# Two attention layers between two long convolutions: a written instruction order per step, one exp over four PSUM banks, turns by DMA and GpSimd, first blocks by predicated copies

## The chip, the cores and the metric

The kernel runs on one core of a Trainium2 chip. The metric is the time of one launch in device microseconds (us), the median over a kernel's runs. Every ratio below is the mean time of one kernel's fast runs over the mean of the other's fast runs of the same rounds, with a 95% interval; it is therefore not quite the ratio of the medians that stand beside it. Shares and durations come from one profiled run of each kernel. The engines are PE (matmul; PEld is its weight load), DVE (vector), ACT (scalar), POOL (GpSimd) and SP (the queue that issues most DMAs).

## The reference, cut to what matters

```python
x = A_u                                             # 1 x 2048 x 512, bf16
x = x + _A_ref(_layernorm(x), A_..., )              # long convolution over 2048 positions
x = x + _B_ref(_layernorm(x), B_wqkv, B_wo)         # attention 1
x = x + _A_ref(_layernorm(x), A_..., )              # the same convolution again
x = x + _B_ref(_layernorm(x), B_wqkv, B_wo)         # attention 2, the same weights

def _B_ref(x, wqkv, wo):
    H = 32; Dh = 16; W, dil = 8, 2                  # each query sees 8 keys, two apart
    q, k, v = split(x @ wqkv)
    logits = q . k[pos - 2*(0..7)] * Dh**-0.5       # masked before position 0
    o = softmax(logits) @ v
    return o @ wo
```

Keys are two positions apart, so even and odd positions never meet. The kernel treats them as two parities. It cuts each parity into blocks of 114 queries against 128 keys, with a mask added in the matmul. One step handles 16 (head, block) pairs, and there are 36 steps in each attention layer.

## The kernel before

One attention layer normalises X, turns it (channels to partitions), projects to K and Q, and then runs 36 steps. A step makes logits on PE, takes exp on ACT, multiplies by V on PE and divides on DVE. Projections for later steps are pulled from a queue during the steps.

```python
def start(g):                       # four row tiles: norm, turn on PE, copy out of PSUM
    for i in range(4):
        ln_b.norm(xn[i][:], X[:, slot(g * 4 + i), :], g * 4 + i)                # DVE, L212
    for ch in range(2):
        pt = gps([128, 4, 2, 128], BF)
        # ... eight nc.tensor.transpose, then copies on ACT and DVE into xnT
def proj(n, k):                     # 512 positions of 128 features of K or Q
    # ... four matmuls of 512 columns (L941), copy to st[n] (L943)
    if h:                           # a DMA spreads st over the two halves of K or Q
        for e in range(2):
            nc.sync.dma_start(T[e::2, e, f2, UF:UF + 1024], st[n][e::2, :])
def logits(t):
    for ih in range(2):
        S4 = psS.tile([128, 2, 512], F32, name="S4", tag="S4")       # two banks, two buffers
        # ... eight matmuls (L968)
        nc.scalar.activation(pt[:, ih*8*NQ:(ih+1)*8*NQ]..., S4[:, :, 0:4*NQ], ACT.Exp, scale=DH**-0.5)   # L971
def values(t):                      # 16 matmuls with V (L985), reciprocal, multiply to on (DVE)
    ...
def turn_o(t):                      # two PE transposes a step, one DVE copy every third step
    ...
for g in range(2): start(g)
for k in range(4): proj(0, k)       # whole first K/Q before the first step
for g in range(2, 4): start(g)
queue = [ ... proj, vproj, out ... ]
for t in range(N + LT):
    logits(t)
    # ... as many jobs of the queue as pace(t) allows
    values(t - 2); turn_o(t - 4)
for m in range(8, 16): out(m)       # output projection; statistics for the next layer per 4 rows
```

The order of instructions on the engines was left to the scheduler here. Convolution 2 began by normalising X into U by groups of four rows, and turned its first blocks (`zt<-Z`) by a DMA transpose.

Of the kernel before, what the change touches and what calls it, by code (L numbers as in the profile page):

```python
# [18 lines left out]
S = 2048  # L19
# [23 lines left out]
HALO = 7  # L43
MASK = 2048.0
# [116 lines left out]
def load_b_weights(nc, const, wq_in, C, wqkv, wo):  # L161
    wqk = const.tile([128, 4, 1024], BF, name="wqk")
    wv = const.tile([128, 4, 512], BF, name="wv")
    wo_t = const.tile([128, 4, 512], BF, name="wo_t")
    wsrc = wqkv.rearrange("(t p) f -> p t f", p=128)
    eng = nc.gpsimd
    mask = nc.inline_tensor(_bf(_mask_rows()), name="c_mask").ap()
    sets = []
    for u in range(2):
        sets.append([const.tile([128, 2, 2, UW], BF, name=f"{nm}{u}") for nm in ("KS", "QS")])  # L170
        for w, T in enumerate(sets[u]):
            nc.gpsimd.memset(T[:, :, :, 0:UF], 0.0)
            nc.gpsimd.memset(T[:, :, :, UF + 1024:UW], 0.0)
            for e in range(2):
                eng.dma_start(T[1 - e::2, e], mask[w].unsqueeze(1).to_broadcast([64, 2, UW]))
        if u == 0:
            for w in range(2):
                for e in range(2):
                    nc.gpsimd.tensor_copy(
                        wqk[:, :, w * 512:w * 512 + 512].rearrange("p t (g d e) -> p e t g d", d=DH, e=2)[:, e],  # L180
                        wq_in[:, :, w * 512:w * 512 + 512].rearrange("p t (g e d) -> p e t g d", d=DH, e=2)[:, e])
            eng.dma_start(wv[:], wsrc[:, :, 1024:1536])
    eng.dma_start(wo_t[:], wo.rearrange("(t p) o -> p t o", p=128))
    return dict(wqk=wqk, wv=wv, wo=wo_t, sets=sets)


class LnStats:


    def __init__(self, nc, pool, parts, nm, eps):  # L190
        self.nc, self.parts, self.eps = nc, parts, eps
        self.st = pool.tile([128, NJ, len(parts), 6], F32, name="ln_st_" + nm)
        self.mv = pool.tile([128, NJ, 2], F32, name="ln_mv_" + nm)
        self.den = pool.tile([128, NJ], BF, name="ln_den_" + nm)
        self.rstd = pool.tile([128, NJ], F32, name="ln_rstd_" + nm)
        self.nb = pool.tile([128, NJ], F32, name="ln_nb_" + nm)

# [5 lines left out]
    def finish(self, j0, j1):  # L203
        nc, js = self.nc, slice(j0, j1)
        for j in range(j0, j1):
            nc.vector.bn_aggr(self.mv[:, j, :], self.st[:, j].rearrange("p a b -> p (a b)"))
        nc.scalar.activation(self.den[:, js], self.mv[:, js, 1], ACT.Sqrt, bias=self.eps[:, 0:1])
        nc.vector.reciprocal(self.rstd[:, js], self.den[:, js])
        nc.vector.scalar_tensor_tensor(self.nb[:, js], self.mv[:, js, 0], -1.0, self.rstd[:, js], ALU.mult, ALU.mult)

# [435 lines left out]
def kernel_and_first_conv(nc, tc, C, prm, x2d, const, kt_dram, kscr, ln, ln_b, W, wq_src):  # L646
    with ExitStack() as es:
# [102 lines left out]
        def after(j0, j1):  # L750
            ln_b.gather(X, 1, j0, j1)
            ln_b.finish(j0, j1)
            marks.append(room(tc, 40))
        with tc.manual_schedule(engines={mybir.EngineType.PE}):
# [13 lines left out]
            ln_b.gather(X, 0, 0, NJ)  # L768
            nc.sync.dma_start(kt_dram[3], Kt[:])
# [4 lines left out]
def a_layer(nc, tc, C, X, kt_dram, ln, ln_b, marks):  # L774

    with ExitStack() as es:
        vpool = es.enter_context(tc.tile_pool(reuse_waits="tile", name="a_vt", bufs=2))
        big = es.enter_context(tc.tile_pool(reuse_waits="tile", name="a_big", bufs=1))
# [7 lines left out]
        U = big.tile([128, NJ, D], BF, name="U")  # L786
# [7 lines left out]
        def s1(k):  # L794
# [10 lines left out]
            nc.scalar.copy(dst, ps[:].rearrange("k r i (j d) -> k (r i) j d", d=8))  # L805

        def turns(k):
            if k % 2 == 0:
# [58 lines left out]
        for q in range(4):  # L867
            with at(tc, marks[q]):
                for j in range(q * 4, q * 4 + 4):
                    ln.norm(U[:, slot(j), :], X[:, slot(j), :], j)  # L870
        marks = []
        for k in range(16 + 13):
# [6 lines left out]
            elif 4 <= q:  # L879
                ln_b.gather(X, 1, (q - 4) * 4, q * 4 - 12)  # L880
                ln_b.finish((q - 4) * 4, q * 4 - 12)
# [4 lines left out]
def b_layer(nc, tc, C, X, Wt, ln_b, marks, store=None, ln_next=None):  # L886

    with ExitStack() as es:
# [4 lines left out]
        psS = es.enter_context(tc.tile_pool(reuse_waits="tile", name="b_psS", bufs=2, space=PSUM))  # L893
        psG = es.enter_context(tc.tile_pool(reuse_waits="tile", name="b_psG", bufs=4, space=PSUM))
        ident = C["ident"]
        wqk, wv, wo_t, sets = Wt["wqk"], Wt["wv"], Wt["wo"], Wt["sets"]
        xnT = big.tile([128, 4, 2, UP], BF, name="xnT")
# [3 lines left out]
        out_marks = []  # L901
        nc.gpsimd.memset(xnT[:, :, :, 0:UF], 0.0)
        nc.gpsimd.memset(xnT[:, :, :, UF + 1024:UP], 0.0)
        nc.gpsimd.memset(V[:, :, :, DH], 1.0)
        for par in range(2):
            nc.gpsimd.memset(V[0:HALO, par * NB, :, DH], 0.0)
        for t in PT:
            nc.gpsimd.memset(t[:, 16 * NQ:], 0.0)
# [4 lines left out]
        def start(g):  # L913
            par, j0 = g // 2, (g % 2) * 4
            xn = []
            for i in range(4):
                xn.append(xnp.tile([128, D], BF, name="xn", tag="xn"))
                ln_b.norm(xn[i][:], X[:, slot(g * 4 + i), :], g * 4 + i)
            for ch in range(2):
                pt = gps([128, 4, 2, 128], BF)  # L920
                for i in range(4):
                    for c in range(2):
                        ct = ch * 2 + c
                        nc.tensor.transpose(pt[:, i, c, :], xn[i][:, ct * 128:(ct + 1) * 128], ident[:])  # L924
                for c in range(2):
                    dst = xnT[:, ch * 2 + c, par, UF:UF + 1024].rearrange("c (p j) -> c p j", j=8)[:, :, j0:j0 + 4]
                    (nc.scalar.copy if par == 0 or c == 0 else nc.vector.tensor_copy)(  # L927
                        dst, pt[:, :, c, :].rearrange("c j p -> c p j"))

        st = {}  # L930

        def proj(n, k):
# [3 lines left out]
            if h == 0:  # L936
                st[n] = stp.tile([128, 1024], BF, name="st", tag="st")
# [5 lines left out]
            (nc.scalar.copy if n == 0 and h == 1 else nc.vector.tensor_copy)(st[n][:, h * 512:h * 512 + 512], ps[:])  # L943
            if h:
                T = sets[n % 2][1 - which]
                for e in range(2):
                    nc.sync.dma_start(T[e::2, e, f2, UF:UF + 1024], st[n][e::2, :])

        def vproj(par, b):
            ps = gps([128, H, DH])  # L950
            for ct in range(4):
                nc.tensor.matmul(ps[:].rearrange("p h d -> p (h d)"), xnT[:, ct, par, NQ * b + 1:NQ * b + 1 + NK],  # L952
                                 wv[:, ct, :], start=(ct == 0), stop=(ct == 3))
            nc.vector.tensor_copy(V[:, par * NB + b, :, 0:DH], ps[:])  # L954

        def logits(t):
# [3 lines left out]
            for ih in range(2):  # L960
                S4 = psS.tile([128, 2, 512], F32, name="S4", tag="S4")
                for x in range(2):
                    f2, b = (t % NB * 2 + x) // NB, (t % NB * 2 + x) % NB
                    for e in range(2):
                        sl = x * 2 + e
                        for i in range(2):
                            r = slice(64 * ih + 32 * i, 64 * ih + 32 * i + 32)
                            nc.tensor.matmul(S4[:, i, sl * NQ:(sl + 1) * NQ], KS[r, e, f2, b * NQ + 1:b * NQ + 1 + NK],  # L968
                                             QS[r, e, f2, UF + b * NQ:UF + b * NQ + NQ],
                                             start=True, stop=True, skip_group_check=True)  # L970
                nc.scalar.activation(pt[:, ih * 8 * NQ:(ih + 1) * 8 * NQ].rearrange("k (i x) -> k i x", i=2),  # L971
                                     S4[:, :, 0:4 * NQ], ACT.Exp, scale=DH ** -0.5)

        ons = {}

        def values(t):
            par, fp = t // NB // 2, t // NB % 2
            pt = PT[t % 3]
            O = gps([128, 16, DH + 1])
            for i in range(4):  # L980
                for sl in range(4):
# [7 lines left out]
            nc.vector.reciprocal(rd[0:NQ], O[0:NQ, :, DH])  # L989
            on = sm.tile([128, 256], BF, name="on", tag="on")  # L990
            nc.vector.tensor_tensor(on[0:NQ].rearrange("q (h d) -> q h d", d=DH), O[0:NQ, :, 0:DH],  # L991
                                    rd[0:NQ].unsqueeze(2).to_broadcast([NQ, 16, DH]), ALU.mult)
            ons[t] = on
# [3 lines left out]
        def turn_o(t):  # L997
            n, s = t // NB, t % NB
            if s % 3 == 0:
                pts[n] = gps([128, 6, NQ], BF)  # L1000
            on = ons.pop(t)
            for x in range(2):
                nc.tensor.transpose(pts[n][:, s % 3 * 2 + x, :], on[0:NQ, x * 128:(x + 1) * 128], ident[0:NQ, 0:NQ])  # L1003
            if s % 3 == 2:
                dst = oT[:, n // 2, n % 2 * 2:n % 2 * 2 + 2, :].rearrange("f t q -> f (t q)")
                nc.vector.tensor_copy(dst[:, (s - 2) * 2 * NQ:(s + 1) * 2 * NQ],
                                      pts[n][:].rearrange("f b q -> f (b q)"))

        def out(m):
            j = slot(m)  # L1010
            par, jp = j % 2, j // 2
            ps = gps([128, 512])
            on_act = m >= 8 and m % 2 == 1
            for ft in range(4):
# [129 lines left out]
```

## Time and profile before

The time was 584.6 us (median of 3 runs, 581.05 to 585.16). The profiled execution took 578.4 us, less than any of the timed ones. I divide the profiled run at the last copy of a convolution's output, the first logits and the last exp of each layer, and the first product of convolution 2 (`xp`).

| stage before | us |
|---|---|
| start to last X copy of convolution 1 | 257.5 |
| prologue of attention 1 (to first logits) | 20.6 |
| 36 steps of attention 1 (to last exp) | 95.1 |
| output tail and start of convolution 2 (to first `xp`) | 24.6 |
| convolution 2 (to last X copy) | 55.8 |
| prologue of attention 2 | 17.9 |
| 36 steps of attention 2 | 92.5 |
| last output tail | 12.8 |

The stretches table of the kernel before has one row for a stretch (from:to, length, then busy us of each engine with its instruction count, the granted clock of PE and the DMA share). The rows below are the two prologues, the two sets of steps, and the start of convolution 2.

```profile
core 0: us, PE busy (x) PEld busy (x) DVE busy (x) ACT busy (x) POOL busy (x), PEclk, DMA share, GB/s
257.50:278.00 20.50, 12.87 (x94) 7.47 (x96) 17.31 (x51) 8.59 (x18) 6.41 (x13) 0.83 0.33 109
278.00:373.20 95.20, 87.11 (x1394) 53.53 (x1414) 63.78 (x151) 69.55 (x80) 0.00 (x0) 0.96 0.12 41
...
383.60:397.80 14.20, 6.08 (x49) 4.34 (x47) 7.22 (x26) 6.08 (x7) 0.00 (x0) 0.73 0.15 29
...
453.50:471.40 17.90, 13.69 (x89) 7.96 (x92) 14.24 (x60) 8.95 (x20) 2.84 (x6) 0.71 0.08 29
471.40:563.90 92.50, 86.99 (x1401) 53.29 (x1420) 60.54 (x134) 64.05 (x75) 0.00 (x0) 1.00 0.15 53
```

In the steps PE is busy 92 to 94% of the time and no other engine comes close, so PE's work sets them. In the prologues and at the start of convolution 2, PE is busy 43 to 77% and often at a lowered clock (0.71 to 0.83 granted in these three). Those are chains of short operations in which each waits for the last.

The costliest groups on the page of the same kernel show what a step is made of (line, engine, operation, out<-in, shapes, count; busy us and mean ns; idle before and its releaser).

```profile
L971 ACT ACTIVATE PT<-S 128x912 bf16<-128x912 f32 x144 | 124.1, 937 | 52.7 <-PE S L968 48.9
L941 PE MATMUL psG<-xnT,wqk 128*128 128x512 bf16 x234 | 65.6, 392 | 2.7 <-ACT xnT L927 0.9
...
L968 PE MATMUL S<-QS,KS 32*128 32x114 bf16 x1152 | 46.4, 212 | 9.6 <-ACT PT L971 6.7
...
L985 PE MATMUL psG<-V,PT 128*128 128x17 bf16 x1152 | 42.5, 171 | 0.3
```

ACT waited 48.9 us for logits; PE waited only 6.7 us for exp. Two details of the timeline: in the prologue of attention 1, a GpSimd fill of V ran at the same time as four norms on DVE (start, length, engine, line).

```profile
260.85 2.55 POOL L904 MEMSET V<- 128x576 bf16 x1
...
259.57 5.13 DVE L212 TENSOR_SCALAR xn<-X,ln_rstd_b,ln_nb_b 128x512 bf16<-128x512 bf16 x4
```

Four norms usually take 4 x 0.40 us; these took 5.13, one of them 4.03. That one began 1.3 us before the fill; what held it so early is not shown. The second detail is the start of convolution 2, where PE waited 4.25 us for the DMA transpose of the first block.

```profile
397.76 0.61 PE L816 MATMUL xp<-zt,sb_C 128*128 128x512 bf16 x1 [4.25 <-DMA zt<-Z]
```

### The profile page before, as it was taken

Reading aid. Unit: us, or ns where it says so; the run is one execution under the profiler, and the core shown is the slowest. Engines: PE = TensorE matmul, PEld = TensorE weight load, DVE = VectorE, ACT = ScalarE, POOL = GpSimd, SP = SyncE. Lnnn points to the kernel's source line nnn. Section 1 sums busy time; section 2 is a strip of 40 time slices with the busy share of each in tenths; the row PEclk is TensorE's granted clock in tenths of the full one; section 3 lists DMA queues with packets and bytes.
Section 4 is the critical chain, followed back from the end, with each engine's and each line's share of the span. In section 5 each row is a group of like instructions: output and inputs, shape, how many; then the busy total and the mean of one; then the engine's idle time right before and its main releaser. Section 6 shows DMA issues by size and latency. Waiting matters only on the chain.

```text
span 576.7 us, 15098 instructions
## 1 busy us (share of the span) xinstructions
PE 415.1 (72%) x6449; PEld 264.4 (46%) x6512; DVE 456.5 (79%) x991; ACT 353.1 (61%) x468; POOL 27.5 (5%) x64
## 2 busy tenths in 40 slices
PE   1101575584694786885999999785997699999896
PEld 0100442362463454643455556543665545555564
DVE  5999999899989987978575767682999956676663
ACT  4999554362564553634767766844996467676472
POOL 0000000000000023413000000000000200000000
PEclk9999997796898877997999999786999689999999
DMA  8201057535633486223101101033672010211122
GB/s 280 93 1 36 2 111 111 93 107 116 84 119 88 88 193 165 68 86 123 58 32 66 54 20 56 3 145 74 165 173 29 1 55 20 76 39 39 56 93 74
DMA packets 76583, 47.51 MB, mean 82 GB/s; under 512 B 62435, under 2 KB 68452, under 8 KB 75236
## 3 DMA queue, kind: packets, MB, share of 16 engines
q1 hardware_dynamic: 74004, 42.74, 29.0%
q0 software_dynamic: 928, 3.41, 1.8%
q8 instruction: 51, 0.84, 0.6%
q10 hardware_dynamic: 1584, 0.39, 0.3%
q14 instruction: 16, 0.13, 0.1%
HBM read 17.96 MB, written 8.13 MB: 45 GB/s over the span
## 4 chain that ended last, share of the span: by engine, by line
PE 29%; ACT 9%; DVE 8%; issue 4%; DMA 2%; SPq 0%; ACTq 0%
PE psG L941 7%; ACT PT L971 6%; PE S L968 5%; PE psG L1015 4%; PE psG L952 4%; PE psG L985 3%; DVE ln_st_b L201 2%; DMA zt<-Z 1%; PE ps_s L802 1%; ACT xc L821 1%; PE psG L1003 1%; DVE ln_st_a L201 1%; ACT Z L805 1%; DMA KS<-st 1%; PE psG L924 1%
## 5 line engine op out<-in xcount | busy, mean ns | idle before, releaser
L971 ACT ACTIVATE PT<-S 128x912 bf16<-128x912 f32 x144 | 124.1, 937 | 52.7 <-PE S L968 48.9
L941 PE MATMUL psG<-xnT,wqk 128*128 128x512 bf16 x234 | 65.6, 392 | 2.7 <-ACT xnT L927 0.9
L943 DVE CAST st<-psG 128x512 bf16<-128x512 f32 x56 | 38.6, 690 | 26.2 <-PE psG L941 24.3
L968 PE MATMUL S<-QS,KS 32*128 32x114 bf16 x1152 | 46.4, 212 | 9.6 <-ACT PT L971 6.7
L985 PEld LDWEIGHTS <-PT 128*128 128x128 bf16 x1152 | 40.0, 96 | 16.4 <-issue 1.9
L954 DVE CAST V<-psG 128x512 bf16<-128x512 f32 x36 | 25.0, 694 | 23.1 <-PE psG L952 22.1
L985 PE MATMUL psG<-V,PT 128*128 128x17 bf16 x1152 | 42.5, 171 | 0.3
L968 PEld LDWEIGHTS <-KS 32*128 32x128 bf16 x1152 | 27.8, 94 | 31.0 <-issue 24.0
L259 PE MATMUL psA<-X,sb_F 128*128 128x128 bf16 x128 | 13.8, 242 | 36.5 <-ACT X L672 35.2
L952 PE MATMUL psG<-wv,xnT 128*128 128x512 bf16 x130 | 35.9, 381 | 1.3 <-issue 0.8
L259 PEld LDWEIGHTS <-sb_F 128*128 128x128 bf16 x256 | 16.2, 102 | 43.1 <-issue 40.5
L941 PEld LDWEIGHTS <-wqk 128*128 128x128 bf16 x256 | 22.7, 100 | 25.2 <-issue 5.4
L1015 PE MATMUL psG<-wo_t,oT 128*128 128x512 bf16 x120 | 32.7, 398 | 0.5 <-issue 0.2
L246 ACT CAST Z<-psA 128x1024 bf16<-128x1024 f32 (+1 forms) x32 | 28.8, 985 | 6.5 <-PE psA L259 6.5
L627 PE MATMUL psk<-Ytab,Xtab 128*32 128x64 bf16 x1024 | 23.5, 206 | 12.4 <-issue 6.6
L991 DVE TENSOR_TENSOR on<-psG,rd 114x256 bf16<-114x256 f32 x72 | 30.1, 419 | 1.7
L284 PE MATMUL psA<-zt,sb_C 128*128 128x512 bf16 x30 | 15.1, 530 | 21.9 <-DMA zt<-Z 21.9
L608 DVE TENSOR_TENSOR Ytab<-Ytab,MA 128x2048 bf16<-128x2048 bf16 (+1 forms) x33 | 30.6, 927 | 0.2
L630 PE MATMUL psk<-Y2tab,Xtab 128*32 128x48 bf16 x1024 | 22.8, 202 | 11.0 <-issue 8.9
L610 DVE TENSOR_TENSOR Y2tab<-Ytab,MB 128x2048 bf16<-128x2048 bf16 (+1 forms) x33 | 30.5, 926 | 0.0
L636 ACT CAST KTq<-psk 128x1024 bf16<-128x1024 f32 (+1 forms) x9 | 8.3, 918 | 32.3 <-issue 31.7
L630 PEld LDWEIGHTS <-Xtab 128*32 128x32 bf16 x1024 | 20.5, 101 | 15.4 <-issue 14.5
(198 smaller groups left out, 1008.9 us busy)
## 6 DMA issues: line engine op xcount, KB each, us to landing
kt_scratch<-Kt SPq DMA_DIRECT2D x4, 1024.0 KB, 3.9
QS<-st SPq DMA_DIRECT2D x32, 128.0 KB, 2.0
KS<-st SPq DMA_DIRECT2D x32, 128.0 KB, 2.0
Kt<-kt_scratch SPq DMA_DIRECT2D x4, 1024.0 KB, 5.9
X<-in_A_u_dram SPq DMA_DIRECT2D x4, 512.0 KB, 5.3
out_dram<-X SPq DMA_DIRECT2D x4, 512.0 KB, 2.9
k_scratch<-KTq SPq DMA_DIRECT2D x7, 256.0 KB, 2.3
KT<-k_scratch SPq DMA_DIRECT2D x7, 256.0 KB, 2.9
```

Of the source, the lines that this page charges most:

```text
L259: nc.tensor.matmul(o, F1[:, j, r, :], rhs_j(j), start=True, stop=not dk)
L608: nc.vector.tensor_tensor(v(Y[:, :, :, q * EYB:(q + 1) * EYB, :]), src, vm(self.mult(self.MA, lev, hc, EYB)), ALU.mult)
L610: nc.vector.tensor_tensor(v(Y2[:, :, :, (q - 1) * EYB:q * EYB, :]), src, vm(self.mult(self.MB, lev, hc, EYB)), ALU.mult)
L630: nc.tensor.matmul(psk[32 * g:32 * g + 32, ds, EYB:], xs, Y2[:, 1 - m // 2, h, :, t], start=False, stop=(m == 3), skip_group_check=True)
L941: nc.tensor.matmul(ps[:], wqk[:, ct, f0:f0 + 128], xnT[:, ct, par, UF + h * 512:UF + h * 512 + 512], start=(ct == 0), stop=(ct == 3))
L943: (nc.scalar.copy if n == 0 and h == 1 else nc.vector.tensor_copy)(st[n][:, h * 512:h * 512 + 512], ps[:])
L952: nc.tensor.matmul(ps[:].rearrange("p h d -> p (h d)"), xnT[:, ct, par, NQ * b + 1:NQ * b + 1 + NK], wv[:, ct, :], start=(ct == 0), stop=( ...
L968: nc.tensor.matmul(S4[:, i, sl * NQ:(sl + 1) * NQ], KS[r, e, f2, b * NQ + 1:b * NQ + 1 + NK], QS[r, e, f2, UF + b * NQ:UF + b * NQ + NQ], ...
L971: nc.scalar.activation(pt[:, ih * 8 * NQ:(ih + 1) * 8 * NQ].rearrange("k (i x) -> k i x", i=2), S4[:, :, 0:4 * NQ], ACT.Exp, scale=DH ** -0.5)
L985: nc.tensor.matmul(O[:, x * 8 + i * 2 + e, :], pt[:, c0:c0 + 128], V[:, par * NB + b, (fp * 2 + f2) * 8 + i * 2 + e, :], start=True, stop= ...
L991: nc.vector.tensor_tensor(on[0:NQ].rearrange("q (h d) -> q h d", d=DH), O[0:NQ, :, 0:DH], rd[0:NQ].unsqueeze(2).to_broadcast([NQ, 16, DH]) ...
L1015: nc.tensor.matmul(ps[:], oT[:, par, ft, 0:1024].rearrange("f (p j) -> f j p", j=8)[:, jp], wo_t[:, ft, :], start=(ft == 0), stop=(ft == 3 ...
```

## The change

The intent is to shorten the latency chains and to relieve PE and ACT in the steps:

- The attention runs in a written order on PE, DVE and ACT instead of the scheduler's.
- One exp per step reads four banks (1824 columns) instead of two of 912. There is one four-bank buffer for logits instead of two two-bank buffers.
- Only the first two of four row groups are normalised and turned on PE before the first step. The other two are normalised in steps 2 and 4, turned by DMA transposes and placed by GpSimd copies. O is turned the same way every third step.
- The first 240 columns of the first K and Q blocks go straight from PSUM by predicated copies; the rest goes by DMA as before.
- The next layer's statistics come from the output add's accumulator and an ACT square. Convolution 2 begins with eight rows already normalised, and turns its first two blocks on PE.
- GpSimd's fills of V and K/Q are moved (`first()`, `second()`).

```diff
 def logits(t):
-            for ih in range(2):
-                S4 = psS.tile([128, 2, 512], F32, name="S4", tag="S4")
+            S = sps([128, 4, 512])
 ...
+            nc.scalar.activation(pt[:, 0:16 * NQ].rearrange("k (i x) -> k i x", i=4), S[:, :, 0:4 * NQ], ACT.Exp,
+                                 scale=DH ** -0.5)
 ... in proj:
+                if early:
+                    for e in range(2):
+                        nc.vector.copy_predicated(T[:, e, f2, UF:UF + FIRST], par_rows[:, e:e + 1].to_broadcast([128, FIRST]),
+                                                  ps[:, 0:FIRST])
 ... in normed (groups 2 and 3):
+                for h in range(2):
+                    nc.sync.dma_start_transpose(xt[:, 8 * h:8 * h + 8], xq[:, 2 * h:2 * h + 2].rearrange("p i d -> p (i d)"))
+                for ct in range(4):
+                    nc.gpsimd.tensor_copy(dst[:, :, (g % 2) * 4:(g % 2) * 4 + 4], xt[:].rearrange(...)[:, ct])
 ... O:
+        def turn_o(g):
+            oS = ld.tile([128, 6, 128], BF, name="oS", tag="oS")
+            nc.sync.dma_start_transpose(oS[:], ons[g][:])
+            nc.gpsimd.tensor_copy(turned_o(g // 3, g % 3 * 3).rearrange("f (b q) -> f b q", q=NQ), oS[:, :, 0:NQ])
 ... the order:
+        with tc.manual_schedule(engines={mybir.EngineType.PE, mybir.EngineType.DVE, mybir.EngineType.Activation}):
+            stats(0); root(0); warm(6)                    # warm: filler matmuls
+            ... norms, turns and copies of groups 0 and 1
+            for k in (0, 2):
+                for _ in proj(0, k, on_act, True): pass   # only two of K/Q's four first projections
+            nc.scalar.activation(pre[:], C["half"][:, 0:1], ACT.Exp)      # loads exp's table
+            jobs = [(0, 2, proj(0, 1, on_act)), (0, 2, proj(0, 3))]       # the other two: in step 0
+            ... every later projection, V block and output row with a step by which it is due
+            for t in range(N):
+                logits(t); square(); work(end - 1)
+                if t >= 2: values(t - 2)
+                work(end)
+                if t >= N - 3: turn_last(t - 3)           # last ones on PE
+                elif t >= 4 and t % 3 == 1: turn_o(t // 3 - 1)
+                if t in (1, 3): stats(2 + t // 2, C["half"])
+                elif t in (2, 4): ... scales and normed of group 1 + t // 2
+            ... the tail:
+                ln_next.root_sums(0, 8, C["half"]); ...; ln_next.scale_sums(0, 8)
+                for m in range(8):
+                    unorm(m, nc.scalar if m < 3 else nc.gpsimd)
+                nc.scalar.activation(pre[:], C["half"][:, 0:1], ACT.Sqrt)
```

## The prediction

> Stages before (timeline, stretches table): first convolution to 255 us; attention 1 prologue to 278, its 36 steps to 373.2, output tail to 383.6; second convolution to 453.5; attention 2 prologue to 471.4, steps to 563.9, tail to 576.7. The first 255 us stay nearly unchanged.
>
> **What bounds it.** The steps: PE is busy 87.1 of 95.2 us and 87.0 of 92.5 us, ACT 64 to 70, DVE 61 to 64; the chain of waits alternates PE lines with exp: 2.57 to 2.64 us a step. In the timeline a step costs PE about 0.61 us (16 value matmuls), 0.19 (turning O), 0.34 (logits), the rest projections at about 0.86 per four 512-column matmuls. The prologues and the 383.6 to 397.8 stretch are latency: PE is busy 14.7 of 23.0, 13.7 of 17.9 and 6.1 of 14.2 us; the chain runs through statistics, norm, transposes, copies, a DMA into K/Q, and a 3.3 us DMA transpose in the second convolution.
>
> **Removed, added, moved.**
> 1. Prologue: only groups 0 and 1 are normalised first; half the copies feed two early projections; the first 240 columns go by predicated copy, not DMA (2.0 us landing). Groups 2 and 3 go later by DMA and GpSimd. From the trace's pieces: statistics 1.3, root and scales 0.7, norms 0.8 to 1.6, transposes and copies of two groups 4, two projections 2, copies 1: first logits about 11 to 12 us after the last convolution copy. Gain 10 us in layer 1, 7 in layer 2.
> 2. Steps: exp goes from 2 x 0.93 to one of 1824 columns; from 1024 columns in 1.02 and 512 in 0.59 us I estimate 1.70. PE loses O's transposes (0.19 a step), gains two projections. PE then needs about 2.35 a step on average. But with one four-bank buffer exp (1.70), logits (0.34) and two handoffs follow each other, about 2.25. So about 2.4 a step, 86 us: gain 9 in layer 1 (which also loses four 1.28 us table loads), 6 in layer 2.
> 3. Start of convolution 2: sums come from the add's accumulator and an ACT square instead of 0.68 us statistics; eight rows are normalised before the tail ends; the first two blocks turn on PE (about 1.7 us against 3.3). Gain 8 us.
> 4. End of convolution 2: DVE loses the small statistics: 1 us. Last tail: 1 us.
>
> Sum about 42 us, nearly all critical; discounted to 38: **546.5 us, 531 to 568**. Faster by over 2% 0.95, within 0.04, slower 0.01.
>
> **GpSimd.** [...] one DVE norm took 4.03 us instead of 0.40 while a 2.55 us GpSimd memset ran. So GpSimd copies should cost nothing in the steps (DVE mostly reads PSUM) but 1 to 3 us at prologues and tail.
>
> **What would show it.** Right: logits under 13 us after the last convolution copy; 144 exp become 72 of about 1.70 us; ACT idle about 0.5 us a step waiting for logits; no 3 us DMA wait at the second convolution's start; U ready within 4 us of the last output add. Wrong: PE waiting on exp over 0.4 us a step, or on K/Q DMAs queued behind DMA transposes; GpSimd's 6.3 us weight copy delaying the first projection.
>
> **What would make it wrong.** The single S buffer locking PE and ACT in step (2.6 a step takes 15 us back), or transposes delaying K/Q.

## The result, and the profile after

The kernel after took 552.69 us (4 runs, 552.11 to 554.43) against 582.83 us (4 runs) of the kernel before in the same rounds: ratio 0.9493, interval 0.9432 to 0.9553. Repeated with the last experiments it took 555.34 us (6 runs, 551.83 to 556.97), ratio 0.9545, interval 0.9494 to 0.9596. The direction and the range were right. The expected value of 546.5 us was 6 us too low. The range was wide, and it held although the predicted terms add up to 42 us and the stages to 25.5. The stages are those of the two profiled executions (578.4 and 553.0 us); the medians lie 30.1 us apart, and the stages cannot place the difference of 4.6.

The same events as before give this account of the profiled runs. They differ by 25.5 us, less than the medians' 30.1, because the kernel before scatters between 579 and 585 us and its profiled run, at 578.4 us, lay at the fast end.

| stage | before | after | change | predicted |
|---|---|---|---|---|
| to last X copy of convolution 1 | 257.5 | 258.6 | +1.1 | 0 |
| prologue 1 | 20.6 | 10.1 | -10.5 | -10 |
| steps 1 | 95.1 | 92.2 | -2.9 | -9 |
| last exp to first `xp` | 24.6 | 20.3 | -4.3 | -8 |
| convolution 2 | 55.8 | 55.6 | -0.2 | -1 |
| prologue 2 | 17.9 | 12.6 | -5.3 | -7 |
| steps 2 | 92.5 | 89.0 | -3.5 | -6 |
| last tail | 12.8 | 12.8 | 0.0 | -1 |
| sum | 576.7 | 551.1 | -25.5 | -42 (discounted to -38) |

The stretches of the kernel after that answer to those shown above are these.

```profile
258.55:268.64 10.09, 6.07 (x51) 3.42 (x52) 6.85 (x21) 7.13 (x12) 3.82 (x7) 1.00 0.55 179
268.64:360.85 92.21, 85.97 (x1443) 54.02 (x1444) 60.30 (x162) 70.54 (x69) 20.14 (x24) 0.96 0.34 78
...
436.67:449.29 12.62, 7.10 (x52) 4.56 (x52) 9.22 (x34) 7.43 (x14) 0.00 (x0) 0.86 0.03 8
449.29:538.32 89.03, 84.34 (x1443) 53.60 (x1444) 58.74 (x154) 65.92 (x53) 18.14 (x22) 0.98 0.43 92
```

PE's work in the steps hardly shrank: 87.1 to 86.0 us in layer 1 and 87.0 to 84.3 in layer 2. The prologues' PE work did shrink, from 94 matmuls in 12.87 us to 51 in 6.07. The groups after:

```profile
L1081 ACT ACTIVATE PT<-S 128x1824 bf16<-128x1824 f32 x72 | 121.8, 1691 | 43.6 <-PE S L1078 43.6
L1036 PE MATMUL psG<-XU,wqk 128*128 128x512 bf16 x256 | 71.0, 394 | 0.2
...
L1097 PE MATMUL O<-V,PT 128*128 128x17 bf16 x1152 | 40.1, 171 | 1.9 <-DVE on L1105 1.9
...
L1078 PE MATMUL S<-QS,KS 32*128 32x114 bf16 x1152 | 29.5, 214 | 15.2 <-DMA KS<-st 5.5
```

The exp takes 1.691 us; the prediction's estimate was 1.70, drawn from ACT's 1024 columns in 1.02 us and 512 in 0.59, and two of 912 columns took 2 x 0.937 us before. The logits' matmuls are busy 17 us less than before (46.4 to 29.5). In the one four-bank tile they go round four groups of 32 rows instead of two; experiment 1, which has two again, shows 36.7 us, so about 7 us of it come with that order, which the prediction had not counted. The time they waited for K by DMA is new.

### Where the steps' gain went

I divided each layer's steps by the start of exp: from the first exp to the eighth (seven steps), to the fourteenth, to the thirty-fourth, and to the end of the last exp.

| us | before, layer 1 | after, layer 1 | before, layer 2 | after, layer 2 |
|---|---|---|---|---|
| last X copy to first exp | 22.6 | 10.5 | 19.3 | 13.0 |
| first seven steps | 16.0 | 24.3 | 16.9 | 22.5 |
| next six | 15.0 | 15.5 | 15.3 | 15.4 |
| next twenty | 54.0 | 45.8 | 53.9 | 44.6 |
| rest, to the end of the last exp | 8.1 | 6.2 | 5.1 | 6.2 |
| last X copy to end of last exp | 115.7 | 102.3 | 110.4 | 101.7 |

The stretches of the first seven steps and of the twenty, before and then after:

```profile
280.04:296.05 16.01, 14.67 (x230) 8.62 (x232) 9.29 (x20) 11.96 (x14) 0.00 (x0) 1.00 0.04 14
311.10:365.08 53.98, 51.48 (x838) 32.23 (x850) 39.21 (x91) 37.66 (x44) 0.00 (x0) 1.00 0.12 41
```

```profile
269.07:293.35 24.28, 20.89 (x267) 11.28 (x266) 16.97 (x51) 13.58 (x12) 8.14 (x10) 0.86 0.45 96
308.88:354.64 45.76, 44.40 (x805) 29.27 (x803) 30.45 (x79) 40.09 (x43) 4.54 (x6) 1.00 0.35 79
```

The twenty steps became 8.2 and 9.3 us shorter, more than a whole layer was predicted to gain from its steps in layer 2, and they run at 2.23 to 2.29 us each. The first seven became 8.3 and 5.6 us longer. Part of this is work that had stood in the prologue. Counted by weight loads, 32 projection matmuls came before layer 1's first exp and 6 in the first seven steps; now it is 10 and 38. (The other matmuls that left the prologue, 32 turns of groups 2 and 3, went to DMA and not to PE; V was not in the prologue before either.) PE's busy time in these steps rose by 6.2 us, but not all of that is work. Experiment 12 below has the same matmuls in these steps at a granted clock of 1.00. The rows are layer 2 before and after, then layers 1 and 2 of experiment 12:

```profile
472.82:489.73 16.91, 16.50 (x239) 9.24 (x241) 9.81 (x21) 12.70 (x16) 0.00 (x0) 1.00 0.10 33
449.72:472.20 22.48, 19.60 (x267) 11.02 (x266) 15.41 (x51) 13.59 (x12) 7.17 (x9) 0.92 0.50 95
...
269.33:289.42 20.09, 18.37 (x267) 10.42 (x266) 18.14 (x54) 13.06 (x11) 6.87 (x8) 1.00 0.47 85
443.61:463.31 19.70, 18.04 (x267) 10.50 (x266) 17.75 (x54) 13.06 (x11) 6.70 (x8) 1.00 0.46 83
```

So of the 8.3 us of layer 1, 3.7 are more PE work (14.67 to 18.37), 2.5 the lower clock (18.37 to 20.89) and 2.1 more idle time of PE. Of the 5.6 us of layer 2 they are 1.5, 1.6 and 2.5. Work moved behind the first logits is thus less than half of what the prologue's gain cost; the rest is clock and waits. At the eighth exp the new kernel is ahead by only 3.8 us in layer 1 (38.57 to 34.80 us from the last X copy) and 0.7 us in layer 2 (36.20 to 35.53).

The lower clock begins like this. PE waited 2.47 us before its first logits and then ran its eight projection matmuls slowly.

```profile
266.60 1.28 ACT L1208 ACT_TABLE_LOAD   x1
...
268.64 0.38 PE L1078 MATMUL S<-QS,KS 32*128 32x114 bf16 x16 [2.47 <-ACT pre L1208]
268.95 2.95 PE L1036 MATMUL psG<-XU,wqk 128*128 128x512 bf16 x8
```

The line names ACT, which was done at 268.10 us. The last two copies out of the turned rows' banks on DVE ended later, at 268.53 (1.28 us from 267.25 on), and the four-bank buffer takes those banks, so the logits had to wait for them. In layer 2 that copy is the releaser named, for 2.43 us. The granted clock was 1.00 from 266 to 268.6 and 0.50 from 270 to 272.

### The profile page after: what moved, and what is told of

The parts are those of the page before. It is cut to its first block, busy times and chain, and to the rows that moved or that the text cites. A ratio compares the mean times of both kernels' runs of the same rounds, so it can differ in the third digit from the quotient of the medians.

```text
span 551.1 us, 15275 instructions
## 1 busy us (share of the span) xinstructions
PE 401.5 (73%) x6528; PEld 258.9 (47%) x6528; DVE 430.4 (78%) x958; ACT 359.6 (65%) x444; POOL 71.0 (13%) x118
## 3 DMA queue, kind: packets, MB, share of 16 engines
q0 software_dynamic: 928, 3.41, 1.9%
## 4 chain that ended last, share of the span: by engine, by line
PE 38%; DVE 21%; ACT 10%; DMA 7%; issue 2%; SPq 2%; ACTq 0%; DVEq 0%
PE psG L1036 10%; DMA zt<-Z 5%; PE psG L1061 4%; PE S L1078 4%; PE O L1097 4%; ACT PT L1081 4%; DVE Ytab L656 3%; DVE Y2tab L658 3%; PE psG L1132 2%; DMA KS<-st 2%; DVE ln_st_b L212 2%; DVE ta L619 2%; ACT xn L241 2%; DVE tb L620 2%; SPq L266 2%
## 5 line engine op out<-in xcount | busy, mean ns | idle before, releaser
L1081 ACT ACTIVATE PT<-S 128x1824 bf16<-128x1824 f32 x72 | 121.8, 1691 | 43.6 <-PE S L1078 43.6
L1036 PE MATMUL psG<-XU,wqk 128*128 128x512 bf16 x256 | 71.0, 394 | 0.2
L1041 DVE CAST st<-psG 128x512 bf16<-128x512 f32 x58 | 39.8, 686 | 28.4 <-PE psG L1036 28.4
L1061 PE MATMUL psG<-wv,XU 128*128 128x256 bf16 x288 | 41.1, 278 | 0.6 <-ACT V L1063 0.6
L1097 PE MATMUL O<-V,PT 128*128 128x17 bf16 x1152 | 40.1, 171 | 1.9 <-DVE on L1105 1.9
L1078 PE MATMUL S<-QS,KS 32*128 32x114 bf16 x1152 | 29.5, 214 | 15.2 <-DMA KS<-st 5.5
L1078 PEld LDWEIGHTS <-KS 32*128 32x128 bf16 x1152 | 20.2, 95 | 40.7 <-issue 29.4
L332 PE MATMUL psA<-zt,sb_C 128*128 128x512 bf16 x30 | 16.4, 574 | 25.2 <-DMA zt<-Z 25.1
L1101 DVE RECIPROCAL rd<-O 128x16 f32<-128x16 f32 x72 | 18.2, 253 | 18.6 <-PE O L1097 17.3
L1105 DVE TENSOR_TENSOR on<-O,rd 128x256 bf16<-128x256 f32 x72 | 30.6, 424 | 2.5
L678 PE MATMUL psk<-Y2tab,Xtab 128*32 128x48 bf16 x1024 | 22.3, 200 | 10.5 <-issue 8.4
L1114 POOL COPY oT<-oS 128x684 bf16<-128x684 bf16 x20 | 15.1, 757 | 105.0 <-DMA oS<-on 105.0
L1061 PEld LDWEIGHTS <-XU 128*128 128x128 bf16 x288 | 25.3, 99 | 7.1 <-issue 1.4
```

The costliest lines, as they stand in the source:

```text
L1036: nc.tensor.matmul(ps[:], wqk[:, ct, f0:f0 + 128], xnT[:, ct, par, UF + h * 512:UF + h * 512 + 512], start=(ct == 0), stop=(ct == 3))
L1041: eng(st[n, which][:, h * 512:h * 512 + 512], ps[:])
L1061: nc.tensor.matmul(ps[:].rearrange("p h d -> p (h d)"), xnT[:, ct, par, NQ * b + 1:NQ * b + 1 + NK], wv[:, ct, fp * 256:fp * 256 + 256], s ...
L1078: nc.tensor.matmul(S[:, i, sl * NQ:(sl + 1) * NQ], KS[r, e, f2, b * NQ + 1:b * NQ + 1 + NK], QS[r, e, f2, UF + b * NQ:UF + b * NQ + NQ], s ...
L1081: nc.scalar.activation(pt[:, 0:16 * NQ].rearrange("k (i x) -> k i x", i=4), S[:, :, 0:4 * NQ], ACT.Exp, scale=DH ** -0.5)
L1097: nc.tensor.matmul(O[:, x * 8 + i * 2 + e, :], pt[:, c0:c0 + 128], V[:, par * NB + b, (fp * 2 + f2) * 8 + i * 2 + e, :], start=True, stop= ...
```

## The experiments

Two theories of the steps stood against each other at first. One said that the single four-bank buffer locks PE and ACT (logits, exp, logits again) at about 2.2 us. The other said that PE's own work fills the step. For the first seven steps the suspects were the statistics and norms of the late groups on DVE, the K/Q DMAs behind transposes on one queue, and the clock. For the tail it was the order on ACT. All twelve kernels gave correct results.

### 1. Two half buffers and two exps again, in the new order

```diff
-            S = sps([128, 4, 512])
+            for ih in range(2):
+                S = sps([128, 2, 512])        # rows 64*ih+32*i, exp of 912 columns each
-            psS = banks("b_psS", 1)
+            psS = banks("b_psS", 2)
```

> The new kernel with its logits back in two tiles of two banks, two buffers, and two exps of 912 columns a step (as before the change); everything else as after. Theory H (hand-over): the light steps 13 to 35 take 2.23 us because the one four-bank buffer makes exp (1.69) and logits plus two hand-overs (0.54) alternate. Then with two buffers these steps fall to 2.0 to 2.1 us, the steps 7 to 12 stay at 2.6, and the time falls by 4 to 8 us from 552.7. Rival P (PE): PE's own work in a light step is already 2.2 us, so the steps stay at 2.2 to 2.3 and the time is the same or up to 4 us longer, since ACT pays 0.17 us more a step.

Measured: 549.95 us, ratio 0.9428 (0.9371 to 0.9486). The interval overlaps that of the kernel after. The twenty steps took 45.84 and 44.22 us against 45.76 and 44.61. In almost the same stretch of layer 1 as above:

```profile
308.90:354.60 45.70, 45.37 (x808) 29.70 (x805) 30.30 (x80) 41.21 (x63) 4.54 (x6) 1.00 0.30 75
```

PE was busy 45.37 of 45.70 us. With the buffer freed, the step did not shrink. In the kernel after, the loop through the single buffer (exp 1.69 plus 0.54 us until the next) takes 2.23 us, and PE is busy 44.40 of 45.76, 2.22 us a step, so taking away the first alone shows nothing. The run is also not a clean removal: with two groups of rows a tile instead of four, its logits keep PE busy 10.3 us in this stretch instead of 7.7. That PE has no slack is what experiment 3 shows. The first logits came earlier (8.57 and 9.79 us after the last X copy, against 10.09 and 12.62), probably since half of the logits no longer wait for the turned rows' last bank. It was given back at once: steps 0 and 1 took 4.5 and 3.0 us, and 4.8 and 4.8 in layer 2.

### 2. Late row groups four steps later

```diff
-                if t in (1, 3): stats(2 + t // 2, C["half"])
-                elif t in (2, 4): g = 1 + t // 2
+                if t in (5, 7): stats((t - 1) // 2, C["half"])
+                elif t in (6, 8): g = t // 2 - 1
```

> Groups 2 and 3 are normalised and turned by DMA in steps 5 to 8 instead of 1 to 4. Theory Q (queue): K/Q stores of the first steps leave the sync queue late behind the DMA transposes (about 1.3 us each); moving four transposes away shortens the steps 0 to 6 (24.4 us in layer 1 and 21.8 us in layer 2) by 1 to 2 us a layer, 2 to 4 us in all. Rival L: the wait is the landing time itself (about 2 us) and PE's projections in those steps, so the time changes by less than 1 us; should the turned groups come too late, step 11 grows by up to 3 us.

Measured: 571.6 us, ratio 0.9806 (0.9756 to 0.9857). The first seven steps took 24.5 and 21.9 us, as with the change itself (24.3 and 22.5), so the late groups' DVE work is not what makes them long. That suspicion fell. The loss is in steps 10 and 11 (8.2 and 4.8 us, and 8.3 and 4.5). The waits of this kernel from 285 to 305 us:

```profile
POOL XU L1002 <- DMA xt<-xq: 8.4, 1, 8.4
DVE ln_rstd_b L230 <- POOL ln_den_b L226: 5.2, 1, 5.2
```

GpSimd took its work in order (its order is still the scheduler's): it stood 8.4 us at a copy that waits for a DMA transpose, and the root of the next group's statistics stood behind that copy. DVE, also in order, waited 5.2 us for the root with V's copies behind it. So here a small operation (the root takes 1.02 us) was as late as the copies queued in front of it. (By the author's account an earlier form, four steps later still, read columns before they were written and was not run.)

### 3. O turned on PE instead of by DMA and GpSimd

```diff
-            nc.sync.dma_start_transpose(oS[:], ons[g][:])
-            nc.gpsimd.tensor_copy(turned_o(...), oS[:, :, 0:NQ])
+            pq = gps([128, 6, NQ], BF)
+            for x in range(6):
+                nc.tensor.transpose(pq[:, x, :], ons[g][0:NQ, x * 128:(x + 1) * 128], ident[0:NQ, 0:NQ])
+            nc.vector.tensor_copy(turned_o(g // 3, g % 3 * 3), pq[:].rearrange("f b q -> f (b q)"))
```

> O is turned on PE again (six transposes and one DVE copy per three steps, at the place of the DMA turn), nothing else changes. Theory P (PE limits the steps): 0.19 us a step come back, light steps go from 2.23 to 2.4 and heavy ones from 2.6 to 2.8, 9 to 12 us longer in all. Theory H (hand-over limits the light steps): PE has slack there and the light steps stay near 2.25; only the twelve heavy steps grow, 3 to 5 us longer in all. If the DMA transposes of O were what held the K/Q stores up, the first seven steps get shorter by 1 us a layer.

Measured: 568.35 us, ratio 0.9745 (0.9688 to 0.9802); the profiled span is 13.9 us longer than that of the kernel after (565.0 against 551.1). Every third step became 0.6 us longer (2.8 instead of 2.2), 0.2 us a step on average. That is what the transposes cost PE before (0.19 us a step in the prediction). The twenty steps took 49.5 and 49.0 us instead of 45.8 and 44.6. In layer 1's twenty PE was busy 47.06 us, 2.7 more than in the kernel after, and 1.4 us it waited for DVE's division before a turn. So PE had no slack to take the turns in. (The copy moved to DVE with them, but DVE is busy only 33.5 of these 49.5 us.) Ten turning steps a layer make about 12 us of the 13.9; the rest lies mostly in layer 2's first seven steps (24.8 us instead of 22.5), whose scatter experiment 4 describes. The turns by DMA and GpSimd are thus worth about 12 us here.

### 4. Two orders in the tail of layer 1

In the kernel after, ACT stood idle after the last exp, then normalised three rows, and only then loaded the table for the root. DVE meanwhile waited for a root that stood behind the squares on ACT, with the last two rows' adds behind it.

```profile
363.78 2.23 ACT L1138 ACTIVATE XU<-X,ln_nb_a,ln_rstd_a 128x512 bf16<-128x512 bf16 x3 [2.93 <-DVE ln_nb_a L256]
366.03 1.28 ACT L1274 ACT_TABLE_LOAD   x1
...
370.71 0.18 DVE L255 RECIPROCAL ln_rstd_a<-ln_den_a 128x4 f32<-128x4 bf16 x1 [2.17 <-ACT ln_den_a L247]
```

```diff
-                for m in range(8): unorm(m, nc.scalar if m < 3 else nc.gpsimd)
-                nc.scalar.activation(pre[:], C["half"][:, 0:1], ACT.Sqrt)
+                nc.scalar.activation(pre[:], C["half"][:, 0:1], ACT.Sqrt)
+                for m in range(8): unorm(m, nc.scalar if m < 3 else nc.gpsimd)
-                    if m == 13: ln_next.scale_sums(8, 12)     # and the norms of rows 8, 9
+                    if m == 15: ln_next.scale_sums(8, 12)     # and the norms of rows 8, 9
```

> In the tail of attention 1 the table load for the root goes in front of the three ACT norms (ACT idles 2.9 us there), and DVE's scales of rows 8 to 11 come after the last output add instead of two adds before it (DVE waited 2.17 us for ACT's root there). Theory O (order): the serial ACT chain of squares and roots sets the start of the second convolution, so last exp to first xp, 20.25 us after the change, gets shorter by 2 to 3 us, and the time by as much. Rival: PE's output matmuls and the copies of Z set it; then under 0.7 us.

Measured: 552.12 us, ratio 0.9471 (0.9424 to 0.9518). From the last exp to the first `xp` it took 18.02 us against 20.25, so the tail gained 2.2 us, and the table load now lies in ACT's wait:

```profile
359.41 1.28 ACT L1272 ACT_TABLE_LOAD   x1
...
362.33 2.23 ACT L1138 ACTIVATE XU<-X,ln_nb_a,ln_rstd_a 128x512 bf16<-128x512 bf16 x3 [1.42 <-DVE ln_nb_a L256]
```

The time as a whole does not prove it by itself, for the intervals overlap. In layer 2's first seven steps this run happened to take 25.4 us instead of 22.5. Those steps scatter from run to run (22.5, 22.6 and 24.6 in kernels that do not touch them). The kept traces show with what: the kernel after and its repeat have one stretch of 3.41 us at a granted clock of 0.50 (half clock) in them (22.5, 22.6), this run and experiment 11 have two (25.4, 24.6). The second lies over step 6, after step 5's wait. Step 6 of layer 2 in the kernel after and in this run:

```profile
469.65:472.20 2.55, 2.55 (x41) 1.33 (x40) 1.87 (x4) 1.69 (x1) 1.82 (x3) 1.00 1.02 204
...
467.12:470.88 3.76, 3.76 (x41) 1.59 (x40) 1.88 (x4) 1.69 (x1) 2.48 (x4) 0.69 0.79 185
```

### 5. Filler matmuls before the first logits

```diff
             nc.scalar.activation(pre[:], C["half"][:, 0:1], ACT.Exp)
+            warm(14)
```

> Fourteen filler matmuls of 272 columns after the two early projections, in PE's 2.4 us of idleness before the first logits; nothing else. Theory C (clock): that idleness lowers the granted clock (0.75 to 0.77 over the first 7 us of steps) and so makes step 0 long: its eight projection matmuls took 2.7 to 3.5 us where 1.75 is usual. Then the clock there is 1.0, step 0 falls from 3.1 to 3.8 us to 2.6, and the fillers delay the first logits by under 0.3 us: 1 to 2 us less in all. Rival W: step 0 is long for other waits, and the fillers only come on top: the same or up to 1 us longer.

Measured: 555.77 us, ratio 0.9566 (0.9526 to 0.9605): no gain in time. The clock theory itself held: with 0.85 us of idleness left, the granted clock stayed at 1.00 from 263 to 272.6 us, where the kernel after, with 2.47 us, had 0.50 from 270 to 272. PE's order in this kernel:

```profile
266.52 0.38 PE L1078 MATMUL S<-QS,KS 32*128 32x114 bf16 x16 [0.85 <-ACT pre L1208]
266.84 1.90 PE L1036 MATMUL psG<-XU,wqk 128*128 128x512 bf16 x8
...
272.24 0.23 PE L1078 MATMUL S<-QS,KS 32*128 32x114 bf16 x4 [1.31 <-DMA KS<-st]
```

The eight matmuls took 1.90 instead of 2.95 us, and step 0 took 2.2 us in both layers. Step 1 then took 4.1 us, because the logits of the next step waited 1.31 us for K by DMA. Steps 0 and 1 together went from 7.3 to 6.3 us in layer 1; in layer 2 they stayed at 6.3, so there the clock's gain was turned into a wait for the stores behind it. Layer 1's first seven steps took 22.4 us (24.3), layer 2's 25.1 (22.5), with a half-clock stretch over step 6 (4.4 us).

### 6. First projections due earlier

```diff
-  due steps of set 0's last four projections: 4, 4, 6, 6 (less 1.5)
+  due steps of set 0's last four projections: 1, 1, 3, 3
-  V block b of set 0 due at step b // 2 + 1
+  V block b of set 0 due at step b // 4 * 2 + 2
```

> Same work per step, other order in the steps 1 to 4 of each layer: the K/Q projections of the set's second half one step earlier, the V projections one step later. Theory D (due too late): step 5 (4.7 to 5.2 us) waits for a K/Q store whose projection ran only in step 4 and which needs about 2 us and a place in the queue; one step earlier takes the wait away: step 5 falls to about 2.7 to 3.0, the first seven steps by about 2 us a layer, 3 to 4.5 us in all. Rival: the wait moves to another step (V late for the value matmuls, or the clock), under 1 us in all.

Measured: 564.76 us, ratio 0.9719 (0.9656 to 0.9782). Step 5, which had waited for K (4.7 and 5.1 us), became 2.6, as the theory says. Step 6 became 9.8 and 8.6 us. The waits of this kernel from 278 to 300 us:

```profile
POOL XU L1002 <- DMA xt<-xq: 14.6, 2, 9.0
...
DVE ln_rstd_b L230 <- POOL ln_den_b L226: 6.2, 1, 6.2
PE psG L1036 <- DVE V L1063: 5.6, 1, 5.6
```

The transposes of the first late group were issued no later than before (22.3 us after the last X copy, against 22.1), and GpSimd's copies of it began only 0.6 us later. What differs is GpSimd's order, which the scheduler sets. In the kernel after, the root of the next late group (L226) came before these copies:

```profile
283.87 1.02 POOL L226 TENSOR_TENSOR ln_den_b<-ln_mv_b,half 128x4 bf16<-128x4 f32 x1
286.25 4.20 POOL L1002 COPY XU<-xt 128x512 bf16<-128x512 bf16 x4 [1.36 <-DMA xt<-xq]
```

Here it stood behind them:

```profile
287.85 4.09 POOL L1002 COPY XU<-xt 128x512 bf16<-128x512 bf16 x4 [9.05 <-DMA xt<-xq]
...
292.30 1.02 POOL L226 TENSOR_TENSOR ln_den_b<-ln_mv_b,half 128x4 bf16<-128x4 f32 x1
```

Its statistics were ready at 285.3 us. GpSimd, DVE and PE waited one behind the other as in experiment 2. So this run shows step 5's cause, but its total says little of the due steps themselves. (The profiled execution, 569.8 us, was the slowest of the four.)

### 7. The second pair of first projections by predicated copies too

```diff
-            jobs = [(0, 2, proj(0, 1, on_act)), (0, 2, proj(0, 3))]
+            jobs = [(0, 2, proj(0, 1, on_dve, 2)), (0, 2, proj(0, 3, on_dve, 2))]
 # and in proj, for early == 2: two copy_predicated of 512 columns, no st copy, no DMA
```

> The second half (columns 512 to 1023) of the first K/Q pair goes by predicated copies too, four of 512 columns on DVE, without copy and DMA store. Theory D2: step 1 (3.1 to 4.1 us) and step 2's logits wait for that store (about 2 us to land); without it step 1 falls to 2.6 to 2.8, 0.7 to 1.3 us less a layer, 1.5 to 2.5 us in all. Rival: DVE's four copies of about 0.7 us, in place of 0.7 of a copy, come as late as the store did, and nothing is gained.

Measured: 551.63 us, ratio 0.9487 (0.9453 to 0.9521). Step 1 went from 3.9 to 2.4 us in layer 1 and from 3.2 to 2.7 in layer 2, so the wait for the K/Q store was its cause. From the last X copy to the end of the last exp it took 100.8 us in both layers, against 102.3 and 101.7. The price is four predicated copies of 0.69 us each a layer, on a DVE that is not the limit there.

### 8. No predicated copies at all

```diff
-                for _ in proj(0, k, on_act, True):
+                for _ in proj(0, k, on_act):
```

> The predicated copies of the first 240 columns are undone: the two early projections are copied whole and go to K and Q by DMA as in the kernel before. Theory: the store's landing (about 2.0 us) and its issue come onto the chain before the first logits, less the predicated copies (about 0.8 us) that go: first logits 1.5 to 2.5 us later per layer, 3 to 5 us longer in all. Rival: the last copies of the turned rows hold the logits' banks as long anyway (they end about 1.2 us after the predicated copies), so the loss is 0.5 to 1 us a layer.

Measured: 559.85 us, ratio 0.963 (0.9582 to 0.9678). In layer 1 the first logits came only 0.6 us later (10.70 against 10.09 us), but now they wait 3.08 us for the DMA, where they had waited 2.47 us for ACT and DVE. In layer 2 they came no later (12.64 against 12.62). The turned rows' banks thus hide most of the DMA, as the rival said. The steps behind lost more than the rival allowed: the time to the end of the last exp rose by 2.6 and 5.4 us. Part of the second number may be the scatter named in experiment 4 (three half-clock stretches in layer 2's first seven steps).

### 9. The kernel after again

> The changed kernel itself, for the comparison within one job: 0.945 to 0.955 of the kernel before, 550 to 555 us, with the first seven steps of a layer between 22 and 26 us from execution to execution.

No edit. Measured: 555.34 us, ratio 0.9545 (0.9494 to 0.9596), beside 552.69 us and 0.9493 in the first rounds. The first seven steps took 24.6 and 22.6 us (24.3 and 22.5 before), so the account above repeats.

### 10. The scheduler's order instead of the written one

```diff
-        with tc.manual_schedule(engines={PE, DVE, Activation}):
+        with ExitStack():
```

> The written order is undone: PE, DVE and ACT of the attention layers are ordered by the framework again, all else as after. Theory A: the written order carries the prologue (two early projections before everything else) and the even spread of background work, so without it the prologues and steps get longer, 8 to 25 us in all. Rival: the program's order is about what the framework finds anyway; within 3 us.

Measured: 562.81 us, ratio 0.9685 (0.9637 to 0.9733), against 0.9545 for the written order in the same rounds. The first logits came 15.9 and 14.1 us after the last X copy (10.1 and 12.7 in the repeat of the kernel after). The first seven steps were shorter than in the written order, 21.3 and 19.8 us (24.6 and 22.6), because the scheduler did more of their work ahead of the first logits (layer 1: 16 projection matmuls instead of 8). The next twenty were longer, 52.8 and 46.0 us (45.8 and 44.6); in layer 1 single late steps took up to 4.8 us. From the last X copy to the end of the last exp the written order gains 8.9 us in layer 1 and loses 0.15 us in layer 2. Its worth is 7.5 us by the medians, a little under the 8 to 25 expected, and it lies in layer 1. This is also the same work found in two places: prologue and first steps together are what counts.

### 11. V's fill back over the norms

```diff
+# second(): V's fill is called in fringe(1), right after KS1's fills; it had run during convolution 1
```

> In attention 1 the 2.57 us GpSimd memset of V, which ran at 242.7 us, is put right after the convolution's end, over DVE's four norms of groups 0 and 1 (0.40 us each, at 258.8 and 261.0). Theory X [...]: one norm is blocked to the memset's end, 1.5 to 2.6 us instead of 0.40, and the first logits of layer 1 come 1 to 2.5 us later (10.1 us after the convolution now); layer 2 stays. Rival: DVE and GpSimd run side by side, norms stay under 0.5 us, no change.

Measured: 558.52 us, ratio 0.9604 (0.9553 to 0.9654); the interval overlaps that of experiment 9, so the total is unclear, but the stage is not. The timeline of this kernel, and then two lines of the kernel after:

```profile
259.14 2.53 POOL L973 MEMSET V<- 128x576 bf16 x1
...
259.49 3.17 DVE L262 TENSOR_SCALAR xn<-X,ln_rstd_b,ln_nb_b 128x512 bf16<-128x512 bf16 x2
```

```profile
242.74 2.57 POOL L970 MEMSET V<- 128x576 bf16 x1 [3.66 <-PE psA L467]
...
258.79 0.73 DVE L260 TENSOR_SCALAR xn<-X,ln_rstd_b,ln_nb_b 128x512 bf16<-128x512 bf16 x2
```

Two norms took 3.17 us beside the fill and 0.73 us without it. The first logits of layer 1 came at 12.40 instead of 10.09 us; those of layer 2, where nothing was moved, stayed at 12.56. Of prologue 1's 10.5 us, 2.3 thus come from the fill's new place, not from the new prologue. At the end of layer 1's last exp 1.2 us of them were left (103.8 against 102.7 us from the last X copy in experiment 9). In the prediction I had named the collision but had not counted the move.

### 12. What held, together

Experiments 4, 5 and 7 together. In addition O is turned one step later (`t % 3 == 2`), and the issuing queue SP is put under the written order.

> Together: the root's table load and scales reordered in the tail (measured 2.2 us of stage), predicated copies for the whole first K/Q pair (1.5 and 0.4 us of steps), fillers before the first logits (step 0 from 3.1 to 3.8 down to 2.2), and the sync queue in written order with O's turn one step later, so that the store of the last first-set projection no longer queues behind a transpose. Theory: the waits of the steps 0 to 6 are clock, store landing and queue, so with all three mended those steps sum to 17 to 19 us (22 to 24 after the change), step 5 falls from about 4.9 to under 3.6, and the time is 541 to 545 us, 7 to 11 us under the changed kernel of the same job. Rival: another wait takes their place and less than 4 us come of it.

Measured: 547.11 us (6 runs, 546.0 to 550.81), ratio 0.9428 (0.9383 to 0.9473), against 555.34 us and 0.9545 for the kernel after in the same rounds; the two intervals do not meet. It has the lowest median of all: 0.9428/0.9545 is 0.988, 1.2% below the kernel after. The gain of 8.2 us is the one expected; the time itself, the first seven steps and step 5 (3.6 and 3.7 us) stayed just above what was named. Experiment 1 had the same ratio in other rounds, and its profiled stages did not account for a gain; the two were not run side by side, nor joined. The first seven steps took 20.1 and 19.7 us (24.3 and 22.5), and the tail to the first `xp` 17.9 us (20.3). Steps 0 and 1 together took 4.9 us in both layers, against 5.9 in experiment 7 without fillers: the fillers, which alone brought layer 2 nothing there, pay once the store behind them is gone. The logits of step 5, which had waited 1.41 us for K in layer 1, waited 0.24. No run takes one of the parts out of this version. Turning O later brought a new wait in step 22 of both layers (4.0 and 3.8 us):

```profile
326.01 0.76 POOL L1120 COPY oT<-oS 128x684 bf16<-128x684 bf16 x1 [5.89 <-DMA oS<-on]
...
326.83 0.44 PE L1138 MATMUL psG<-wo_t,oT 128*128 128x512 bf16 x1 [1.29 <-POOL oT L1120]
```

The first output projection of the layer comes before its turned O is placed. Starting the outputs a step later should save that; it was not tried.

## Why the prediction was right or wrong, point by point

**The bound: right.** The prediction said that PE's work sets the steps. PE busy 44.40 of 45.76 us in the regular twenty steps, and 0.6 us more in each step that got its turns back (experiment 3), show it. Experiment 1 agrees (45.37 of 45.70 us), but its logits cost PE more. The fear that the single buffer would lock PE and ACT at 2.6 us a step was wrong: its loop is at most 2.23 us. The two limits lie so close that less PE work alone may not shorten the step; that was not tested.

**Prologues: the moment was right, its worth was not.** First logits came at 10.09 and 12.62 us, under the 13 us named, and the table of stages shows -10.5 and -5.3 for -10 and -7. But 2.3 us of the first are the moved fill. The gain is not kept either: at the eighth exp 3.8 and 0.7 us remain of it. The first logits are a marker in a chain, not the end of a cost.

**Steps: the step of the prediction that failed.** It read "So about 2.4 a step, 86 us: gain 9 in layer 1 ..., 6 in layer 2". Its parts were right: exp 1.691 for 1.70 us, ACT's wait 0.54 for "about 0.5", 72 for 144 exps. Even PE's total was right: the estimate of 2.35 a step is 84.6 us, and 86.0 and 84.3 were measured. What failed is spreading that total evenly over 36 steps. The regular twenty ran at 2.23 to 2.29 us, better than 2.4. The first seven ran at 3.47 and 3.21 us: the projections that left the prologue have to be done there, at a lowered clock (0.86 and 0.92 granted) and with waits for K/Q stores. Against the kernel before that is 3.7 and 1.5 us of PE work, 2.5 and 1.6 of clock, 2.1 and 2.5 of idle PE. The term measured -2.9 and -3.5 instead of -9 and -6. The moved work had been booked as a gain in the prologue and as a part of an average in the steps; clock and waits had not been booked at all.

**Start of convolution 2: right mechanism, wrong size.** U was ready 3.90 us after the last output add (8.12 before; "within 4" was said), and no 3 us wait for a DMA transpose stood there: from the last first-stage product of the first channel block to the first `xp` it took 4.58 us instead of 5.95. But the tail in front grew from 10.42 to 11.46 us, because ACT received squares and norms in front of a root that DVE then waited for (2.17 us). The term is -4.3 instead of -8. Experiment 4 got 2.2 of the missing 3.7 back by order alone; the rest stays unassigned.

**Convolution 2's end and the last tail: about nothing for 2.** Convolution 2 measured -0.2, the last tail 0.0. Convolution 2 took 53.6 to 57.2 us in the profiles, so 1 us there cannot be told.

**GpSimd: right.** Experiment 11 shows one collision of a fill with two norms at 2.44 us (3.17 less 0.73). For the steps the trace of the kernel after shows the difference that the prediction made: DVE's casts out of PSUM (L1041, 512 columns) had a median of 0.69 us in the 24 that overlapped a GpSimd operation and in the 34 that did not, while four norms, which read SBUF, took 2.87 us beside GpSimd's copies (from 285.66 us on) and 1.38 us without (from 279.74 us on). The weight copy did not delay the first projection (0.2 us idle in that group). What the prediction missed of GpSimd is not its speed but its order: experiments 2 and 6, about 16 and 9 us slower than 555.34, lost most of it to one small operation that the scheduler had put behind a waiting copy.

**K/Q behind transposes: named as a risk, and it came true in part.** The logits waited 5.5 us in all for K, 3.1 us of it between 268 and 290 us. The waits that experiment 7 removed had no transpose in front of them: the stores were issued from 271.3 us on, the first transpose at 280.7. In step 5 one had: K's store was issued at 286.7 us, after O's transpose at 285.3. With O's turn a step later (experiment 12) step 5 took 3.6 us instead of 4.7.

**Open.** Step 3 of both layers takes 3.3 to 3.4 us in most versions in the written order, and no experiment was aimed at it. Layer 2's first seven steps scatter between 22.5 and about 25 us in kernels that do not touch them, with the half-clock stretches of experiment 4; where these fall differs from execution to execution, and one profile of each kernel cannot say how often.

## What to carry to other kernels

When a change moves the first event of a loop forward, measure to a point well inside the loop, since work moved behind the marker is paid there, and so were the waits (2.1 and 2.5 us) and the lower clock (2.5 and 1.6 us) that followed. Where an order is fixed, whether written or set by the scheduler, follow for every small operation what stands in front of it on its engine, above all GpSimd and the DMA queue: in experiments 2 and 6 a root of 1.02 us stood behind copies that had waited 8.4 and 9.0 us for a DMA, and DVE waited 5.2 and 6.2 us for it. When one repair only turns the gain into the next wait, keep it and repair the next: layer 2's steps 0 and 1 took 6.3 us with 5 alone, 5.9 with 7 alone and 4.9 with both.

## What single operations took here

- The clock: in the kernel after, PE's gap of 2.47 us before layer 1's first logits ended at 268.64 us, and the granted clock was 0.50 for 3.41 us, from 269.66 to 273.07. With 14 filler matmuls (0.85 us idle left) it stayed at 1.00.
- DMA transposes (128 x 768 and 128 x 1024 bf16 within SBUF) mostly held the issuing queue for about 1.25 us each, and landed 2.8 to 4.9 us after issue.
- ACT's table load took 1.28 us. The one of 266.60 us began 0.01 us after ACT's last copy, and the next ACTIVATE began 0.02 us after its end.
- GpSimd's power operation took 1.02 us for 128x4 and 1.63 us for 128x8.
- The predicated copy from PSUM on DVE took 0.40 us for 240 columns and 0.69 us for 512, as long as a plain copy of 512 columns with a cast (0.69 us).
